# Attention, then two expert layers, on one Trainium2 core: a product's place in the planned order no longer waits for its reciprocals

## The chip, the core and the metric

One core of a Trainium2 chip runs the whole program. PE (TensorE) multiplies, DVE (VectorE), ACT (ScalarE) and POOL (GpSimd) work on tiles, SP (SyncE) issues most transfers. Each engine runs its own instructions in the order in which the program names them. The metric is the device time of one execution in microseconds, the median of the runs.

## The reference

```python
def _attn_ref(q, k, v, tau):          # q, k, v: 4 batches x 8 heads x 576 x 64
    scores = np.matmul(q, k.transpose(0, 1, 3, 2)) / sqrt(64)
    thresh = np.max(scores, axis=-1, keepdims=True) - tau
    scores = np.where(scores >= thresh, scores, -1000000000.0)
    attn = np.exp(scores - np.max(scores, axis=-1, keepdims=True))
    attn = attn / (np.sum(attn, axis=-1, keepdims=True) + 1e-09)
    return np.matmul(attn, v)
def _moe_ref(x, w1, w2, w3, w_out):   # x: 2304 x 512, w1, w2: 512 x 1024
    return ((x @ w1) * (x @ w2) @ w3) @ w_out
def _moe2_ref(x, w_in, w_out):        # w_in: 512 x 2048
    h = x @ w_in
    g = np.where(h > 0.0, h, np.exp(np.minimum(h, 0.0)) - 1.0)
    return g @ w_out
```

The output of the attention, laid out as 2304 tokens of 512 numbers, goes through `_moe_ref`, and that through `_moe2_ref`.

## The kernel before

**Pairs and score tiles.** The 32 heads go in 16 pairs p. The scores of a pair are nine tiles i of 128 rows by 576 columns: positions 0 to 3 make half 0 of the pair (256 rows), positions 4 to 8 half 1 (320 rows), so there are 144 tiles and 32 halves. A name such as `s75` is the score tile 75, and `pv8_1` is the product of pair 8, half 1. Pairs 0 to 3 ("plain") go in another form (L478) and do all their first halves ahead of their second ones.

**A tile's way.** PE makes the scores (`emit_S`, L478 or L490) into one of three PSUM slots `s`. DVE takes each row's maximum (`emit_max`, L500), POOL makes the threshold and the bias of it, ACT the exponential `e` (`emit_exp`, L518), and DVE masks it and sums the rows (`emit_mask`, L524). Then the tile is transposed, in one of two ways, into a buffer `pt` of the half; there are two such buffers. Either PE transposes it back into its own slot and ACT copies that out (`emit_X`, L572; `emit_C`, L576), or ACT and POOL split it into two f16 parts `hl` (L531, L535) and SP starts DMA transposes (`emit_T`, L562 and L564). The second way is taken by second halves from pair 4 on, and by odd pairs below, and by first halves from pair 10 on.

**A half's way.** When its tiles are masked, DVE adds 1e-9 to the row sums and takes reciprocals (`emit_rr`, L584 and L585). PE turns them (`turn_r`, L590, in the slot of the tile named `q + 3` in the code), ACT copies them out (`keep_r`, L595), SP stores them to DRAM (`store_r`, `rd`) and loads them back spread over 64 partitions each (`load_rs`, L615, tile `rb`). When the half's `pt` is full, PE multiplies it with V (`emit_PV`): twelve of the 32 products are in f32 (L629, ten matmuls, each of which the profile counts twice), twenty in f16 (L637, 28 matmuls). DVE multiplies the product with `rb` (`emit_xf`, L646 or L648), ACT and DVE split the result into two parts of x (`emit_xh`, L654; `emit_xl`, L658). The product itself reads V and `pt` only; `rb` is first read by `emit_xf`.

**The first layer's products.** As soon as four pairs of a batch have their x, PE makes `ab` products of them with w1 and w2 (`run_ab`, L679, twelve matmuls each), which ACT (L687) and DVE (L694) evict. Batches 0 to 2 do this among the score tiles; the fourth follows after them. The `ab` products and the products with V share two PSUM banks `m`: a half holds one from the first matmul of its product until `emit_xf`.

**What sets the order.** All of this stage, up to about 420 us, is put in order by a class `Plan`. Each step is an operation with an engine, a modelled duration, a list of steps that must come first, and a key. `run` takes, again and again, the engine that could begin earliest, and on it, among the steps that could begin within `SLACK` of the earliest one, the one with the lowest key. The table `AHEAD` shifts the keys by kind of step and stretch. A step named in a list is thus an entry in the planner's book: the program issues the instructions in the order found, and the semaphores on the chip follow from what each instruction reads and writes, not from the list. The later stages (the matrix M of w3 and w_out, x, h and o with the ELU) are written by hand.

Of the kernel before, what the change touches and what calls it, by code (L numbers as in the profile page):

```python
# [50 lines left out]
SLACK = {"PE": 0.03, "DVE": 0.02, "ACT": 0.05, "POOL": 0.31, "SP": 0.44, "NEW": 0.05}  # L51
AHEAD = {
    ("emit_C", 0, 0): 224.5, ("emit_C", 0, 1): 627, ("emit_C", 1, 1): -173.5, ("emit_C", 1, 2): -182.5,
    ("emit_C", 2, 3): -166, ("emit_C", 2, 4): 48, ("emit_C", 2, 5): -140, ("emit_C", 2, 6): -180,
    ("emit_C", 2, 7): -322, ("emit_H", 1, 1): -184, ("emit_H", 1, 2): -253.5, ("emit_H", 2, 3): 1130,
    ("emit_H", 2, 4): 882, ("emit_H", 2, 5): 1110, ("emit_H", 2, 6): 608.5, ("emit_H", 2, 7): 900,
    ("emit_H", 2, 8): 425, ("emit_H", 2, 9): 950, ("emit_H", 2, 10): 910, ("emit_H", 2, 11): 1090,
    ("emit_L", 1, 1): -91.5, ("emit_L", 1, 2): 43, ("emit_L", 2, 3): 177, ("emit_L", 2, 4): 56.5,
    ("emit_L", 2, 5): 160, ("emit_L", 2, 6): -46.5, ("emit_L", 2, 7): 41.5, ("emit_L", 2, 8): -58,
    ("emit_L", 2, 9): 87.5, ("emit_L", 2, 10): 112, ("emit_L", 2, 11): 316.5, ("emit_PV", 0, 0): -405.5,  # L60
    ("emit_PV", 0, 1): 54.5, ("emit_PV", 0, 2): 23, ("emit_PV", 0, 3): 25, ("emit_PV", 0, 4): -0.5,
    ("emit_PV", 0, 5): 3.5, ("emit_PV", 0, 6): -23.5, ("emit_PV", 0, 7): 76.5, ("emit_PV", 1, 0): -28,
    ("emit_PV", 1, 1): 10.5, ("emit_PV", 1, 2): -84.5, ("emit_PV", 1, 3): -121, ("emit_PV", 1, 4): 2,
    ("emit_PV", 1, 5): -28.5, ("emit_PV", 1, 6): -81.5, ("emit_PV", 1, 7): -16.5, ("emit_S", 0, 0): -362,
    ("emit_S", 0, 1): 20, ("emit_S", 1, 1): -165.5, ("emit_S", 1, 2): -129.5, ("emit_S", 2, 3): -0.5,
    ("emit_S", 2, 4): -255.5, ("emit_S", 2, 5): -113.5, ("emit_S", 2, 6): -27.5, ("emit_S", 2, 7): -3.5,
    ("emit_S", 2, 8): -1.5, ("emit_S", 2, 9): -56, ("emit_S", 2, 10): 5.5, ("emit_S", 2, 11): -116.5,
    ("emit_T", 1, 1): 500.5, ("emit_T", 1, 2): 652.5, ("emit_T", 2, 3): -45.5, ("emit_T", 2, 4): 197,
    ("emit_T", 2, 5): -118.5, ("emit_T", 2, 6): 79.5, ("emit_T", 2, 7): 259.5, ("emit_T", 2, 8): 173,
    ("emit_T", 2, 9): 41.5, ("emit_T", 2, 10): 77.5, ("emit_T", 2, 11): -12, ("emit_X", 0, 0): -360,  # L70
    ("emit_X", 0, 1): -68, ("emit_X", 1, 1): -66.5, ("emit_X", 1, 2): -29.5, ("emit_X", 2, 3): -76.5,
    ("emit_X", 2, 4): -192.5, ("emit_X", 2, 5): -99.5, ("emit_X", 2, 6): -308, ("emit_X", 2, 7): -600,
    ("emit_bias", 0, 0): -141, ("emit_bias", 0, 1): 38, ("emit_bias", 1, 1): -277.5, ("emit_bias", 1, 2): -117,
    ("emit_exp", 0, 0): 154, ("emit_exp", 0, 1): 164.5, ("emit_exp", 1, 1): 53.5, ("emit_exp", 1, 2): -83,
# [192 lines left out]
def attention_moe_moe2(  # L267
# [14 lines left out]
    V, A, G, T, SP = nc.vector, nc.scalar, nc.gpsimd, nc.tensor, nc.sync  # L282
# [442 lines left out]
    call = partial  # L725
# [4 lines left out]
    for i in range(NTILE + 4):  # L730
        p, pos = SEQ[i] if i < NTILE else (NPAIR - 1, 0)
# [745 lines left out]
```

## Time and profile before

| | us |
|---|---|
| runs | 1002.31, 998.86, 996.26 |
| median | 998.86 |
| profiled execution | 1000.01 |
| its span | 998.2 |
| PE busy in the span | 965.1 |

The span is the stretch that the profiler recorded, and 1.8 us of the profiled execution lie around it. PE is busy for nearly all of it, so the time outside of PE's work is 33 us, and most of what remains to be had lies in PE's waits. A timeline row says when a run of like instructions began and how long it took, and in brackets how long the engine was idle ahead of it and what released it.

### The profile page before, as it was taken

The page shows a single profiled execution, that of the slowest core. Times are in us where ns is not written, and L with a number is a line of the kernel's source. Part 1 is how long each engine was busy: PE and PEld are TensorE (multiplying, and loading weights), DVE is VectorE, ACT ScalarE, POOL GpSimd, SP SyncE. Part 2 cuts the span into 40 slices and gives each one's busy share as a digit, 9 for nine tenths or more (in the row PEclk, how much of TensorE's full clock was granted, in tenths as well). Part 3 has the DMA queues.
Part 4 walks back from the last instruction along what each step waited for, and adds up shares of the span by engine and source line. Part 5 has one row for each costly group of instructions (what it writes and reads, how often), then busy time and mean ns, then how long its engine had stood idle before and what let it go on. Part 6 is the DMA issues. An engine that isn't in the chain of part 4 may idle for free. (4 is left out here: it accounts for less than half of the span.)

```text
span 998.2 us, 17869 instructions
## 1 busy us (share of the span) xinstructions
PE 965.1 (97%) x6102; PEld 846.8 (85%) x6102; DVE 719.2 (72%) x1235; ACT 562.5 (56%) x1045; POOL 627.7 (63%) x765
## 2 busy tenths in 40 slices
PE   8889999989999999999999999999999999999998
PEld 5547788768898999999899998898989999899997
DVE  6988876878768878499876664788676656765563
ACT  5777786777666776255444344545555344553442
POOL 3378775776779887255422224878887566875662
PEclk9999999989999999999999999999999999999999
DMA  8437565566898988677758866731215121142201
GB/s 269 149 104 191 137 162 168 147 143 158 186 184 189 200 169 173 180 260 255 244 178 263 291 219 195 257 106 54 64 50 195 57 69 53 49 133 58 69 22 64
DMA packets 182263, 152.51 MB, mean 153 GB/s; under 512 B 119484, under 2 KB 168860, under 8 KB 177564
## 3 DMA queue, kind: packets, MB, share of 16 engines
q1 hardware_dynamic: 178060, 121.72, 45.4%
q10 hardware_dynamic: 4112, 29.66, 8.4%
q8 instruction: 48, 0.79, 0.3%
q14 instruction: 43, 0.35, 0.1%
HBM read 98.89 MB, written 24.72 MB: 124 GB/s over the span
## 5 line engine op out<-in xcount | busy, mean ns | idle before, releaser
L679 PE MATMUL ab<-x,W 128*128 128x256 f32 (+1 forms) x1536 | 223.9, 298 | 3.5 <-ACT a L687 1.7
L1306 PE MATMUL o<-W,gg 128*128 128x512 f32 x864 | 222.8, 390 | 0.0
L679 PEld LDWEIGHTS ab<-x,W 128*128 128x128 f32 x1536 | 207.7, 188 | 12.9 <-issue 6.5
L1215 POOL TENSOR_TENSOR wi<-wr,wi 128x256 fp32r<-128x256 f32 x168 | 144.5, 873 | 65.7 <-ACT wi L1214 53.3
L1306 PEld LDWEIGHTS o<-W,gg 128*128 128x128 f32 x864 | 159.9, 188 | 21.5
L1294 POOL TENSOR_TENSOR gg<-th,gg 128x384 fp32r<-128x384 f32 x96 | 106.4, 1108 | 47.0 <-PE h L1346 26.6
L535 POOL TENSOR_TENSOR hl<-e,hl 128x512 f16<-128x512 f32 x94 | 110.1, 1172 | 30.5 <-ACT hl L531 26.7
L524 DVE SCALAR_TENSOR_TENSOR e<-s,st,e 128x576 f32<-128x576 f32 x144 | 115.1, 809 | 17.5 <-ACT e L518 15.7
L500 DVE TENSOR_REDUCE st<-s 128x1 f32<-128x576 f32 x144 | 106.1, 750 | 19.2 <-PE s L490 8.8
L1346 PE MATMUL h<-sl,wi 128*128 128x384 f32 x576 | 116.6, 338 | 2.3 <-DVE th L1376 1.4
L1288 ACT ACTIVATE et<-et 128x384 f32<-128x384 f32 x96 | 50.1, 522 | 111.8 <-DVE et L1287 111.3
L1346 PEld LDWEIGHTS h<-sl,wi 128*128 128x128 f32 x576 | 102.5, 188 | 11.5 <-DVE th L1376 2.3
L1225 PE MATMUL x<-sl,M 128*128 128x384 f32 x576 | 100.6, 336 | 1.4 <-DVE sl L324 1.4
L1225 PEld LDWEIGHTS x<-sl,M 128*128 128x128 f32 x576 | 99.8, 188 | 2.1 <-DVE sl L324 2.0
L1293 ACT ACTIVATE gg<-th 128x384 fp32r<-128x384 f32 x96 | 50.6, 527 | 77.4 <-DVE th L1291 76.8
L1376 DVE TENSOR_TENSOR th<-h,th 128x384 f32<-128x384 f32 x96 | 53.2, 554 | 56.5 <-PE h L1346 56.3
L1346 PE MATMUL h<-so,wi 128*128 128x384 f32 x432 | 87.4, 337 | 2.4 <-ACT th L1386 1.6
L518 ACT ACTIVATE e<-s,st 128x576 f32<-128x576 f32 x108 | 78.2, 735 | 20.4 <-POOL st L508 14.4
L490 PE MATMUL s<-qk 128*128 128x288 f32 x480 | 84.1, 309 | 4.7 <-DVE e L524 2.5
L1346 PEld LDWEIGHTS h<-so,wi 128*128 128x128 f32 x432 | 76.6, 188 | 10.6 <-ACT th L1386 3.6
L1291 DVE SCALAR_TENSOR_TENSOR th<-et,th 128x384 f32<-128x384 f32 x96 | 72.0, 750 | 16.8 <-ACT et L1288 15.4
L490 PEld LDWEIGHTS s<-qk 128*128 128x128 f32 x480 | 68.9, 191 | 13.6 <-issue 5.1
(113 smaller groups left out, 1515.5 us busy)
## 6 DMA issues: line engine op xcount, KB each, us to landing
wr<-wi_dr SPq DMA_DIRECT2D x168, 128.0 KB
rqk<-in_qk SPq DMA_DIRECT2D x24, 576.0 KB
raw_wo<-in_wo ACTq DMA_DIRECT2D x12, 1024.0 KB
th<-g_dr SPq DMA_DIRECT2D x48, 192.0 KB
raw_w<-in_w SPq DMA_DIRECT2D x8, 1024.0 KB
raw_w<-in_w3t ACTq DMA_DIRECT2D x8, 1024.0 KB
raw_win<-in_win ACTq DMA_DIRECT2D x8, 1024.0 KB
vr<-in_v SPq DMA_DIRECT2D x16, 320.0 KB
```

What stands on the lines that cost most here:

```text
L490: T.matmul(s[:, n, :HS], q, k[:, c:c + HS], start=(x == 0), stop=(x == len(ops) - 1))
L500: V.tensor_reduce(st[i][:, 0:1], sc[i][:, :, :HS], axis=AX.XY, op=ALU.max if plain else ALU.min, negate=plain)
L518: A.activation(et[i], sc[i][:, :, :HS], AF.Exp, bias=st[i][:, k:k + 1], scale=esc if plain else -1.0)
L524: V.scalar_tensor_tensor(et[i], sc[i][:, :, :HS], st[i][:, 1:2], et[i], op0=ALU.is_ge if p < NPL else ALU.is_le, op1=ALU.mult, accum_out=s ...
L535: G.tensor_tensor(t[:, S + 64:], e[:, :512], t[:, :512], op=ALU.subtract)
L679: T.matmul(o[:, :w], wf[:, m, wx, kt, :], x[:, xx, :], start=(kt == 0 and k == 0), stop=(kt == NK - 1 and k == 2),)
L1215: G.tensor_tensor(t[:, 1], r, f32(t[:, 0]), op=ALU.subtract)
L1225: T.matmul(o[:, :TB], M[:, f, mx, e * P:(e + 1) * P], gh[j, f][:, gx, :], start=(k == 0), stop=(k == 23),)
L1291: V.scalar_tensor_tensor(x, c["t"], -1.0, x, op0=ALU.add, op1=ALU.max)
L1294: G.tensor_tensor(h[:, 1, :], x, f32(h[:, 0, :]), op=ALU.subtract)
L1306: T.matmul(po[j, t], dst["h"][:, gx, t * P:(t + 1) * P], WO[f][:, wx, :], start=(first and k == 0), stop=(last and k == 2),)
L1346: T.matmul(o[:, :TB], w[:, wx, kt, :], bs[k][:, kt, xx, :], start=(i == 0), stop=(i == 5),)
```

## The change

One dependency is dropped and the numbers that set the order are searched anew. In the loop over the halves, the first step of `emit_PV` listed `lr`, the spread load of the reciprocals of that half; it no longer does. `emit_xf` still lists it. `SLACK` is zero now for PE, DVE and ACT, larger for POOL and smaller for SP, and nearly every number of `AHEAD` differs; one entry is dropped. No instruction is added or removed.

```diff
-SLACK = {"PE": 0.03, "DVE": 0.02, "ACT": 0.05, "POOL": 0.31, "SP": 0.44, "NEW": 0.05}
+SLACK = {"PE": 0.0, "DVE": 0.0, "ACT": 0.0, "POOL": 0.36, "SP": 0.33, "NEW": 0.05}
 AHEAD = {
...
-    ("emit_L", 2, 9): 87.5, ("emit_L", 2, 10): 112, ("emit_L", 2, 11): 316.5, ("emit_PV", 0, 0): -405.5,
+    ("emit_L", 2, 9): 140.5, ("emit_L", 2, 10): 241.5, ("emit_L", 2, 11): 247.5, ("emit_PV", 0, 0): -449,
...
         pv = v0 = op(
-            call(emit_PV, p, n, 0), VV[p, n] + [x for i in tiles for x in CC[i]] + lr + pvs[-1:], "PE", us[0], q + 5
+            call(emit_PV, p, n, 0), VV[p, n] + [x for i in tiles for x in CC[i]] + pvs[-1:], "PE", us[0], q + 5
         )
```

The instructions move in the stage up to about 420 us, on every engine; from there on the order is the same. The table is a line longer, so a line of the kernel before has a number one higher in the changed kernel. In the rows below a name ends in a running number of the build, which means nothing; `<-` stands between what is written and what is read, and `x4` counts like rows.

On PE, at pair 5: the product `pv5_0`, `ab` products of batch 0, half 1, and transposes of tile 56. Before:

```order
L572 MATMUL s56_1998<-ident_116,e56_2060 128x128 x4
L572 MATMUL s56_1998<-ident_116,e56_2060 64x128
L679 MATMUL ab0_1_3_1_2085<-x0_1_977,W3_578 128x320 x3
L679 MATMUL ab0_1_3_1_2085<-x1_1_1258,W3_578 128x320 x3
L679 MATMUL ab0_1_3_1_2085<-x2_1_1422,W3_578 128x320 x3
L679 MATMUL ab0_1_3_1_2085<-x3_1_1638,W3_578 128x320 x3
L629 MATMUL pv5_0_2102<-pt5_0_1731,vr5_1016 64x256 x10
```

Changed:

```order
L638 MATMUL pv4_1_1839<-pt4_1_1563,v16_4_1167 64x320
L630 MATMUL pv5_0_1927<-pt5_0_1712,vr5_1114 64x256 x4
L491 MATMUL s54_1938<-qk8_742 128x288 x4
L630 MATMUL pv5_0_1927<-pt5_0_1712,vr5_1114 64x256 x2
L491 MATMUL s55_1956<-qk8_742 128x288 x4
L630 MATMUL pv5_0_1927<-pt5_0_1712,vr5_1114 64x256 x4
L491 MATMUL s56_1975<-qk9_889 128x288 x4
L680 MATMUL ab0_1_1_1_1984<-x0_1_1106,W1_373 128x320 x3
```

The product has moved from behind `ab0_1_3_1` and tile 56's transposes to right behind `pv4_1`, in three pieces among the score tiles 54 to 56, and so ahead of five `ab` products.

On DVE, at tile 75, which is the fourth tile of pair 8, half 0: maxima, masks and the reciprocals `rr8_0`. Before:

```order
L500 TENSOR_REDUCE st76_2769<-s76_2753 128x1
L500 TENSOR_REDUCE st77_2773<-s77_2764 128x1
L524 SCALAR_TENSOR_TENSOR e75_2771,sm8_2673<-s75_2738,st75_2760,e75_2771 128x576
L524 SCALAR_TENSOR_TENSOR e76_2778,sm8_2673<-s76_2753,st76_2769,e76_2778 128x576
L524 SCALAR_TENSOR_TENSOR e77_2783,sm8_2673<-s77_2764,st77_2773,e77_2783 128x576
L584 TENSOR_SCALAR rr8_0_2795<-sm8_2673 128x4
```

Changed:

```order
L501 TENSOR_REDUCE st76_2764<-s76_2754 128x1
L525 SCALAR_TENSOR_TENSOR e75_2766,sm8_2659<-s75_2739,st75_2759,e75_2766 128x576
L501 TENSOR_REDUCE st77_2778<-s77_2769 128x1
L585 TENSOR_SCALAR rr8_0_2785<-sm8_2659 128x4
L586 RECIPROCAL rr8_0_2785<-rr8_0_2785 128x4
L525 SCALAR_TENSOR_TENSOR e76_2776,sm8_2659<-s76_2754,st76_2764,e76_2776 128x576
```

The mask of tile 75 now stands ahead of the maximum of tile 77, and the reciprocals ahead of two masks.

On SP, behind the load `rb10_1`: `rqk26` is a load of 576 KB of q and k for a later pair, `hl99` to `hl104` are tiles of pair 11 to be transposed. Before:

```order
L615 DMA rb10_1_3782<-rd10_1_3703 64x320 x2
L394 DMA rqk26_3804<-in_qk 128x1152
L564 DMA_TRANSPOSE pt11_0_3808<-hl99_3716 128x9x128
L564 DMA_TRANSPOSE pt11_0_3808<-hl100_3742 128x9x128
L564 DMA_TRANSPOSE pt11_0_3808<-hl101_3814 128x9x128
```

Changed:

```order
L616 DMA rb10_1_3788<-rd10_1_3704 64x320 x2
L565 DMA_TRANSPOSE pt11_0_3740<-hl99_3752 128x9x128
L565 DMA_TRANSPOSE pt11_0_3740<-hl100_3786 128x9x128
L565 DMA_TRANSPOSE pt11_0_3740<-hl101_3809 128x9x128
L607 DMA rd11_0_3910<-rt11_0_3894 4x128
L565 DMA_TRANSPOSE pt11_0_3740<-hl102_3839 128x9x128
L565 DMA_TRANSPOSE pt11_1_3872<-hl103_3887 128x9x128
L616 DMA rb11_0_3954<-rd11_0_3910 64x256 x2
L699 DMA g_dr_67<-g1_0_0_3811 128x2x256
L565 DMA_TRANSPOSE pt11_1_3872<-hl104_3922 128x9x128
L395 DMA rqk26_3999<-in_qk 128x1152
```

The large load has moved behind six transposes, a store and the spread load of the next half.

## Rows read from the trace of the kernel before

**Rows 1.** The page, part 1: engine, busy us (share of the span), instructions.

```profile
PE 965.1 (97%) x6102; PEld 846.8 (85%) x6102; DVE 719.2 (72%) x1235; ACT 562.5 (56%) x1045; POOL 627.7 (63%) x765
```

**Rows 2.** Windows: stretch; length, busy us (instructions) by engine; PEclk, DMA share, GB/s.

```profile
12.00:32.00 20.00, 18.66 (x139) 11.92 (x137) 17.41 (x32) 15.17 (x22) 7.34 (x17) 1.00 0.70 221
...
52.00:72.00 20.00, 16.33 (x124) 9.10 (x123) 16.74 (x33) 15.59 (x23) 12.93 (x18) 1.00 0.36 119
550.00:1000.00 450.00, 438.38 (x2231) 398.44 (x2229) 288.79 (x441) 210.50 (x469) 288.51 (x286) 1.00 0.34 110
```

**Rows 3.** Tile rb, 10 to 420: what ended idle time (us, times).

```profile
  PE pv L637: 9.0, 8
  PE pv L629: 4.1, 4
  DMA rb<-rd: 1.7, 1
```

**Rows 4.** Timeline, DVE: start, length, line, operation, [idle before <- releaser].

```profile
23.67 0.76 DVE L500 TENSOR_REDUCE st<-s 128x1 f32<-128x576 f32 x1 [1.58 <-PE s L590]
```

**Rows 5.** Timeline, PE: product of pair 0, first half.

```profile
32.69 2.53 PE L629 MATMUL pv<-pt,vr 128*64 128x256 f32 x20
```

**Rows 6.** Timeline, ACT, 160 to 240: copies into pt.

```profile
168.34 1.90 ACT L576 ACTIVATE pt<-s 128x640 f32<-128x640 f32 x3 [4.33 <-PE pv L629]
...
189.99 0.70 ACT L576 ACTIVATE pt<-s 128x640 f32<-128x640 f32 x1 [1.71 <-PE pv L629]
```

**Rows 7.** Timeline, PE, 170 to 200: two waits of score tiles.

```profile
177.05 1.86 PE L490 MATMUL s<-qk 128*128 128x288 f32 x12 [1.02 <-ACT pt L576]
...
192.70 0.80 PE L490 MATMUL s<-qk 128*128 128x288 f32 x4 [0.59 <-ACT pt L576]
```

**Rows 8.** Timeline, PE, 204 to 232: products 6_1 and 7_1, and between.

```profile
204.91 2.09 PE L637 MATMUL pv<-pt,v 128*64 128x320 f16 x28
...
217.06 1.33 PE L572 MATMUL s<-ident,e 128*128 128x128 f32 x5 [1.58 <-DVE e L524]
...
220.41 0.47 PE L637 MATMUL pv<-pt,v 128*64 128x320 f16 x1 [0.61 <-DMA pt<-hl]
221.58 3.89 PE L637 MATMUL pv<-pt,v 128*64 128x320 f16 x27 [0.69 <-DMA pt<-hl]
225.40 3.18 PE L490 MATMUL s<-qk 128*128 128x288 f32 x16
```

**Rows 9.** Timeline, DVE: the third maximum of pair 8.

```profile
215.51 0.76 DVE L500 TENSOR_REDUCE st<-s 128x1 f32<-128x576 f32 x1 [0.30 <-PE s L490]
```

**Rows 10.** Windows: one stretch.

```profile
220.00:225.00 5.00, 3.89 (x28) 3.09 (x28) 1.77 (x3) 1.88 (x4) 4.14 (x6) 0.50 0.75 227
```

**Rows 11.** Timeline, PE: behind the second hole.

```profile
300.10 1.69 PE L679 MATMUL ab<-x,W 128*128 128x256 f32 x12 [1.71 <-ACT a L687]
302.97 2.67 PE L490 MATMUL s<-qk 128*128 128x288 f32 x16 [1.18 <-DVE e L524]
```

**Rows 12.** Timeline, SP: load of rb10_1, then transposes.

```profile
289.97 1.12 SPq L615 DMA_DIRECT2D rb<-rd  x2
...
292.19 6.77 SPq L564 DMA_TRANSPOSE pt<-hl  x3
```

**Rows 13.** Timeline, DVE: xf of product 10_1.

```profile
293.85 0.55 DVE L648 SCALAR_TENSOR_TENSOR xf<-pv,vst,rb 128x320 f32<-128x320 f32 x1 [1.74 <-DMA rb<-rd]
```

**Rows 14.** Timeline, ACT: a copy to f16 (hl).

```profile
298.59 0.68 ACT L531 ACTIVATE hl<-e 128x576 f16<-128x576 f32 x1 [4.25 <-DMA pt<-hl]
```

**Rows 15.** Timeline, PE, 380 to 420: two waits of pairs 14 and 15.

```profile
398.19 1.30 PE L490 MATMUL s<-qk 128*128 128x288 f32 x8 [0.53 <-DVE e L524]
...
416.63 3.64 PE L679 MATMUL ab<-x,W 128*128 128x320 f32 x23 [0.65 <-DVE xf L648]
```

**Rows 16.** Timeline, PE: turn_r of product 9_0.

```profile
244.61 0.27 PE L590 MATMUL s<-ident,rr 128*4 128x128 f32 x1
```

**Rows 17.** Timeline, SP: load of rb9_0.

```profile
247.10 1.10 SPq L615 DMA_DIRECT2D rb<-rd  x2
```

More of the change, by code (lines that the diff above doesn't have):

```diff
@@ new lines @@
+    ("emit_tiny", 0, 1): -24, ("emit_tiny", 1, 1): -204.5, ("emit_tiny", 1, 2): -384, ("emit_tiny", 2, 3): -389.5,
+    ("emit_tiny", 2, 4): -146.5, ("emit_tiny", 2, 5): -193.5, ("emit_tiny", 2, 6): -263.5,
+    ("emit_tiny", 2, 7): -283.5, ("emit_tiny", 2, 8): -390, ("emit_tiny", 2, 9): -500.5,
+    ("emit_tiny", 2, 10): -482.5, ("emit_tiny", 2, 11): 95, ("emit_xf", 0, 0): 313.5, ("emit_xf", 0, 1): 405,
+    ("emit_xf", 0, 2): -228.5, ("emit_xf", 0, 3): -40.5, ("emit_xf", 0, 4): -212.5, ("emit_xf", 0, 5): -127.5,
@@ new lines @@
+    ("emit_xf", 0, 6): -254.5, ("emit_xf", 0, 7): 650, ("emit_xf", 1, 0): 64.5, ("emit_xf", 1, 1): -49,
+    ("emit_xf", 1, 2): 40.5, ("emit_xf", 1, 3): 315, ("emit_xf", 1, 4): 227.5, ("emit_xf", 1, 5): 182,
+    ("emit_xf", 1, 6): 157, ("emit_xf", 1, 7): 272, ("emit_xh", 0, 0): -299.5, ("emit_xh", 0, 1): -105,
+    ("emit_xh", 0, 2): 189.5, ("emit_xh", 0, 3): -414.5, ("emit_xh", 0, 4): -597, ("emit_xh", 0, 5): -625,
+    ("emit_xh", 0, 6): -344.5, ("emit_xh", 0, 7): -101.5, ("emit_xh", 1, 0): -120.5, ("emit_xh", 1, 1): 292,
@@ new lines @@
+    ("load_rs", 1, 3): -106.5, ("load_rs", 1, 4): -121.5, ("load_rs", 1, 5): 31, ("load_rs", 1, 6): 164,
+    ("load_rs", 1, 7): -116, ("load_v", 0): -202, ("load_w", 0): -532, ("low", 0): 488.5, ("new_pt", 0): -547,
+    ("prep_h", 0): -633.5, ("prep_lk", 0): 665, ("prep_lq", 0): -226.5, ("prep_s", 0): 390.5, ("prep_v", 0): 263,
+    ("prep_vl", 0): 188.5, ("rest", 0): 418, ("run_ab", 0, 0): -72, ("run_ab", 0, 1): -47, ("run_ab", 0, 2): 49,
+    ("run_ab", 0, 3): 103.5, ("run_ab", 0, 4): 256.5, ("run_ab", 0, 5): 27, ("run_ab", 0, 6): 166.5,
@@ new lines @@
+    ("run_ab", 0, 7): 41, ("run_ab", 1, 0): 118, ("run_ab", 1, 1): 16.5, ("run_ab", 1, 2): -102,
+    ("run_ab", 1, 3): 59, ("run_ab", 1, 4): 187, ("run_ab", 1, 5): 39.5, ("run_ab", 1, 6): -64.5,
+    ("run_ab", 1, 7): 9.5, ("run_ab", 2, 0): 287.5, ("run_ab", 2, 1): -207.5, ("run_ab", 2, 2): -33,
+    ("run_ab", 2, 3): 134, ("run_ab", 2, 4): -285.5, ("run_ab", 2, 5): 9.5, ("run_ab", 2, 6): -93,
+    ("run_ab", 2, 7): 88, ("sign", 0): 428.5, ("store_g", 0, 0): -200.5, ("store_g", 0, 1): -9.5,
+    ("store_g", 0, 2): -142, ("store_g", 0, 3): -43, ("store_g", 0, 4): 100.5, ("store_g", 0, 5): -52,
@@ new lines @@
+    ("store_r", 0, 2): -480, ("store_r", 0, 3): -416.5, ("store_r", 0, 4): -46, ("store_r", 0, 5): -37,
+    ("store_r", 0, 6): -483.5, ("store_r", 0, 7): -216, ("store_r", 1, 0): -207.5, ("store_r", 1, 1): 111.5,
+    ("store_r", 1, 2): -531, ("store_r", 1, 3): -247.5, ("store_r", 1, 4): 97, ("store_r", 1, 5): -441,
+    ("store_r", 1, 6): -458.5, ("store_r", 1, 7): -199.5, ("top", 0): 433.5, ("turn_r", 0, 0): -627,
+    ("turn_r", 0, 1): -138.5, ("turn_r", 0, 2): -643, ("turn_r", 0, 3): -181, ("turn_r", 0, 4): -128,
@@ L147 @@
+    ("turn_r", 0, 5): -285.5, ("turn_r", 0, 6): -384, ("turn_r", 0, 7): -171, ("turn_r", 1, 0): -384.5,
+    ("turn_r", 1, 1): -221, ("turn_r", 1, 2): -249.5, ("turn_r", 1, 3): -380.5, ("turn_r", 1, 4): -51,
+    ("turn_r", 1, 5): -416, ("turn_r", 1, 6): -275.5, ("turn_r", 1, 7): -386.5, ("v_mean", 0): -549.5,
+    ("v_scale", 0): -338.5, ("v_sum", 0): 154,
 }
```

157 lines of the change are left out of this document (64 added, 93 removed).

## The prediction

> **What bounds the kernel now.** I read the page's busy times first. PE works 965.1 of the span's 998.2 us, DVE 719.2 [rows 1]: the kernel is bound by PE as a whole, and 33.1 us are left in which PE waits. Next, the windows, since an average over stages hides where those 33.1 us are. From 550 to 1000, where the later layers run and the change moves nothing, PE is busy 438.38 of 450, so 11.6 of them lie out of reach. In the attention stage the picture has two parts. From 12 to 72 DVE is the fuller beside PE: in the first 20 us DVE works 17.41 and PE 18.66, in the last 16.74 and 16.33 [rows 2]; PE idles 1.34 and 3.67 us there, and the chain scores, maximum, exponential, mask, transpose sets the pace. After that PE is close to full, and what it loses is in a few holes of 1 to 3 us, which the timelines show one by one. Last, the tile `rb`, which is the one the dropped dependency is about: DVE, at `emit_xf`, waited for a product with V twelve times, 13.1 us in all, and for the reciprocals once, 1.7 us [rows 3]. So in the old order the reciprocals are nearly always there first, and the product is the late one. This is the room that the change can use: a product could start sooner without `emit_xf` having to wait at once.
>
> **What the edit does and doesn't do.** The product never reads `rb`, so no semaphore goes away on the chip; the instructions are the same in number and form, and removal and addition cost nothing. All effect is order. By the two orders, 24 of 32 products stand earlier on PE, mostly by one to four score tiles, seven stand as before, and `pv0_1` stands later. SP's, ACT's and POOL's instructions shift with them, and the new table moves others that have nothing to do with it. I go through the places where PE waits in the old trace and ask of each what stands there now. All terms are against the profiled execution, 1000.01; it lies 1.15 above the median of the runs, 998.86, and since the terms are differences I put them on the median.
>
> **Early part, 12 to 72.** `pv0_0` stood behind tile 10's scores and is now ahead of tile 6's; `pv1_0` to `pv3_0` move likewise. One such product takes 2.53 us [rows 5]. Ahead of `s6` it can delay the maximum of tile 6, for which DVE waited 1.58 us even before [rows 4]; that DVE time is lost for good in a stretch paced by DVE, so the cost is at most the whole 2.53. The other end: products placed earlier fill waits of PE there, at best about half of the 1.34 and 3.67 us of the first and last window, 2.5. No row tells which prevails, since PE's work is the same and DVE has 2.6 and 3.3 us of idle in those windows to absorb a delay. I take **0**, ends −2.5 and +2.5.
>
> **Pairs 5 and 6, 165 to 193.** ACT's copies into `pt` stood 4.33 and 1.71 us behind `pv5_0` and `pv6_0` [rows 6], since there are two `pt` buffers and a copy needs the one that the product still reads. Two later score tiles waited 1.02 and 0.59 for such copies [rows 7]. `pv5_0` now stands five `ab` products earlier and `pv6_0` three and a half `ab` products and two score tiles earlier, so the buffers come free in time. What is late next is DVE, which has few gaps here. Between 0 and −1.6 I take half, **−0.8**.
>
> **Pairs 7 and 8, 214 to 228.** PE waited 1.58 for the mask of tile 75, then 0.61 and 0.69 inside `pv7_1` for transposes to land [rows 8], and the granted clock fell to 0.50, which is 1.2 of 2.4 GHz [rows 10]. On DVE the maximum of tile 77, 0.76 us, stood ahead of that mask and had itself waited 0.30 [rows 9]; the new order puts the mask first, so 0.76 can go. On PE `s79`, four matmuls of 0.80 like the one of [rows 7], now stands ahead of `pv7_1` and fills the first wait, 0.61. But the last transpose lands where it did unless SP is faster, and then the earlier mask only lengthens the wait for it. So: 0.61 and half of 0.76, **−1.0**, ends 0 and −1.4, with the clock falling as before.
>
> **Pairs 10 and 11, 291 to 303.** SP issued a 576 KB load and right behind it three transposes that took 6.77 us [rows 12]; ACT's next copy into `hl` waited 4.25 for them [rows 14], and the eviction of an `ab` product is queued behind that copy on ACT: PE waited 1.71 for it, then 1.18 for a mask [rows 11]. The load now stands behind six transposes. On SP nothing else of it is urgent, as its pair is two pairs away. I take the first wait as gone and the second as staying, because DVE's chain is late next: **−1.7**, ends 0 and −2.9.
>
> **Pairs 14 and 15.** PE waited 0.53 for a slot behind a mask and 0.65 for the last `emit_xf` [rows 15]. `pv14_1` now stands ahead of `s143` and can fill the first, `pv15_1` stands four `ab` products earlier and can remove the second. 0.65 and half of 0.53: **−0.9**, ends 0 and −1.2.
>
> **New waits.** A product that is issued sooner can meet a transpose that has not landed, or a bank that is kept. The nearest row for the first is `pv7_1`, 0.61 and 0.69 [rows 8]. I count one such place, **+1.3**, ends 0 and +4.3 (that place and two bank waits of 1.5, worked out below).
> On this place PE's row shows that score matmuls queued behind `pv7_1` began only when it was through, at 225.40, though their inputs are not the product's [rows 8]. The Trainium skill (TensorE: Matmul & The Clock Gate, Step-by-step: what each phase is for) gives the rule: matmuls stay in program order and only weight loads are pulled ahead. By that rule an early product is no free filler, which speaks against this change; a PE that took the scores first would make this term 0 instead.
>
> **Sum.** 0 − 0.8 − 1.0 − 1.7 − 0.9 + 1.3 = −3.1 us. On the profiled execution 996.9, on the median **995.8**, which is 0.3% faster. A measurement of this kernel can tell about 0.5% from no change, 5.0 us, so the bounds are 993.9 and 1003.9. With its two widest terms at either end the forecast runs from 992.0 to 1001.3; I think 993 to 998 likely.
>
> **Rival A, the clock stays up, 991.1.** If all of 1.58, 0.61 and 0.69 is filled, the hole at 217 is gone, and perhaps the fall of the clock with it. The fall's price is in the rows: `pv7_1` took 0.47 and 3.89 where `pv6_1`, as many matmuls, took 2.09, so 2.27; sixteen score matmuls took 3.18 there [rows 8] and 2.67 at 303 [rows 11], so 0.51. That is 2.8 on top, and the hole gives 2.88 instead of 1.0: 995.8 − 1.9 − 2.8 = 991.1. For it: the places that hold PE here are just the ones that moved. Against it: the landing of the transpose is not moved much, and at 300 PE waited 1.71 and 1.18 with no fall, so the clock does not simply follow one wait. The Trainium skill (same page, What's actually happening) says the throttled clock is the default and activity releases it, which fits a fall behind waits and would come out as this rival if they go. Chance 0.22.
>
> **Rival B, waits only change places, 998.9.** The change does not do what it says it does for time: DVE sets the pace early, `emit_xf` that waited for a product now waits for `rb`, and each filled hole opens one of its size behind it. For it: DVE's shares [rows 2] and that the new table moves much that has nothing to do with products. Against it: 12 of the 13 waits at `rb` were for the product [rows 3]. Chance 0.18.
>
> **Rival C, banks are kept for reciprocals, 1004.9.** The old dependency made sure that a product takes one of the two banks only when its reciprocals are on the way. Take `pv9_0` in the new order: behind `turn_r` stand 4 of 28 matmuls of `pv8_1` (0.30 of the 2.09 in [rows 8]), 3 of 12 of an `ab` product (0.42 of 1.69, [rows 11]), two score tiles (1.60, [rows 7]) and the product (2.53, [rows 5]): it ends 4.85 after `turn_r`. The reciprocals take longer: `turn_r` at 244.61 [rows 16], the load's issue over at 248.20 [rows 17], and up to 2.76 until it lands, by the one time that `emit_xf` waited for it (293.85, [rows 13], against an issue over at 291.09, [rows 12]). That is 6.35, so `emit_xf` waits 1.5 and keeps the bank. By the same count six products past 72 us end within 7 us of their `turn_r` (`pv2_1`, `pv6_0`, `pv9_0`, `pv12_1`, `pv13_0`, `pv14_0`); in the old order each began over 6.6 after it. If each costs PE the 1.74 of the one measured wait [rows 13], that is 10.4; with the four gains of 4.4 lost in it, +6.0. It decides from about six such waits on, (5.0 + 4.4) / 1.74. Against it: while one bank is kept PE has scores to do, and the other bank. Chance 0.15.
>
> **How the numbers follow.** The forecast has 0.45, of which I put 0.08 below 993.9. Faster by over 0.5%: 0.22 of rival A and 0.08, 0.30. Slower by over 0.5%: rival C, 0.15. Within 0.5%: the rest of the forecast and rival B, 0.55. The range should leave out two in ten: from 990.0, just under rival A, where a little of it falls short, to 1003.0, which leaves out most of rival C.
>
> **What would show it.** In the changed profile: ACT's copies near 168 and 190 without their waits of 4.33 and 1.71; tile 75's transpose on PE right behind the scores and `pv7_1` in one piece or with one wait; ACT's 4.25 near 298 gone; at tile `rb`, `emit_xf` released by `rb` several times instead of once, which is the sign of rival C where PE's `ab` rows then show waits for DVE's `xf`. A granted clock of 1.00 through 214 to 228 would mean rival A. The prediction is wrong if PE's busy time changes, which only the clock can do, or if new waits in the early part exceed 2.5.

## The result

The changed kernel takes 1010.05 us, median of six runs, against 999.15 for before in the same session: the ratio is 1.0121, interval 1.0100 to 1.0143. It is 11 us slower, where 3 us faster was forecast. The profiled execution took 1014.23, so its trace shows some 4 us more than the median does; it is set against before's trace, 1000.01.

The page of the changed kernel, part 1, answers [rows 1]:

```profile
PE 969.8 (96%) x6102; PEld 851.7 (84%) x6102; DVE 717.3 (71%) x1235; ACT 563.4 (56%) x1045; POOL 627.6 (62%) x765
```

The span is 1012.4. PE is busy 4.7 us longer with the same instructions, and the time in which it waits has grown from 33.1 to 42.6, by 9.5; the two make the 14.2 us. The windows of the changed kernel show where PE's clock fell (columns as in [rows 2]; the last three are PEclk, DMA share, GB/s):

```profile
0.00:50.00 50.00, 40.31 (x273) 25.13 (x274) 38.59 (x75) 29.90 (x44) 19.30 (x40) 0.97 0.60 188
50.00:100.00 50.00, 45.20 (x316) 29.04 (x316) 39.72 (x73) 34.41 (x50) 34.30 (x51) 0.93 0.51 146
...
150.00:200.00 50.00, 47.86 (x353) 40.75 (x353) 37.71 (x83) 36.50 (x62) 34.05 (x53) 0.97 0.67 162
200.00:250.00 50.00, 45.84 (x359) 37.93 (x359) 38.91 (x86) 36.48 (x61) 34.41 (x54) 1.00 0.65 160
...
300.00:350.00 50.00, 44.52 (x354) 41.83 (x354) 30.64 (x69) 27.92 (x52) 34.76 (x53) 0.93 0.83 166
350.00:400.00 50.00, 47.30 (x391) 43.46 (x387) 37.19 (x84) 34.77 (x62) 42.95 (x65) 0.97 0.77 175
```

Before had one fall in this stage, from 217 to 227 [rows 10]. That one is gone, 200 to 250 reads 1.00, and five others have come: in windows of 2 us the clock is low from 46 to 54, 74 to 78, 158 to 164, 322 to 330 and 354 to 358. PE's waits over 0 to 520 (what waited, for what: us in total, times, longest), of before:

```profile
PE s L572 <- DVE e L524: 5.0, 6, 1.6
PE s L478 <- ACT pt L576: 4.4, 7, 1.3
PE s L490 <- DVE e L524: 2.5, 5, 1.2
...
PE s L490 <- ACT pt L576: 1.9, 3, 1.0
PE ab L679 <- ACT a L687: 1.7, 1, 1.7
PE pv L637 <- DMA pt<-hl: 1.3, 2, 0.7
...
PE ab L679 <- DVE g L694: 1.0, 2, 0.5
PE ab L679 <- DVE xf L648: 0.6, 1, 0.6
PE s L478 <- DVE e L524: 0.5, 1, 0.5
```

and of the changed kernel, whose line numbers are one higher:

```profile
PE s L573 <- DVE e L525: 8.9, 8, 2.5
PE pv L638 <- DMA pt<-hl: 3.7, 7, 0.8
PE s L479 <- ACT pt L577: 3.5, 7, 0.8
PE pv L638 <- DMA rqk<-in_qk: 3.4, 1, 3.4
...
PE pv L638 <- DVE st L501: 2.0, 1, 2.0
PE pv L638 <- ACT a L688: 2.0, 2, 1.7
PE s L491 <- DVE e L525: 1.7, 5, 0.6
PE pv L638 <- DVE e L525: 1.5, 1, 1.5
PE s L491 <- ACT pt L577: 1.1, 2, 0.8
...
PE ab L680 <- DVE g L695: 0.5, 1, 0.5
```

Added up by what waited: products with V 1.3 before and 12.6 now, transposes on PE 5.0 and 8.9, scores 9.3 and 6.3, `ab` products 3.3 and 0.5. That is +11.3, +3.9, −3.0 and −2.8, or +9.4, the whole growth of the idle time. The releasers of the five kinds of product waits differ. The 2.0 us put down to ACT may be waits for a bank, which its evictions of `ab` products free. For the others, a wait for several things is put down to the one that came last by the profile, and a product reads no mask, no maximum and not that load, which is for a later pair; the places, below, point to the transposes. At tile `rb` the new trace reads (answering [rows 3]):

```profile
  PE pv L638: 5.8, 5
  DMA rb<-rd: 1.7, 3
  PE pv L630: 0.5, 2
```

`emit_xf` waited for reciprocals three times, 1.7 us in all, as much as in the one wait of before. So the loss is not there.

The three products that lost most are in PE's timeline of the changed kernel. First `pv4_1`, whose first six matmuls stand ahead of the scores of tile 51:

```profile
156.89 0.30 PE L638 MATMUL pv<-pt,v 128*64 128x320 f16 x1 [1.52 <-DVE e L525]
157.81 0.59 PE L638 MATMUL pv<-pt,v 128*64 128x320 f16 x5 [0.62 <-DMA pt<-hl]
158.33 0.80 PE L491 MATMUL s<-qk 128*128 128x288 f32 x4
```

Then `pv11_1` and `pv12_1`, in the same timeline further on:

```profile
324.00 4.43 PE L638 MATMUL pv<-pt,v 128*64 128x320 f16 x28 [3.40 <-DMA rqk<-in_qk]
...
354.00 3.96 PE L638 MATMUL pv<-pt,v 128*64 128x320 f16 x28 [2.00 <-DVE st L501]
```

Scores are queued behind each of them. Next, the last transposes of `pv4_1`'s half, tile 44, in SP's timeline of before (start, length of the issue):

```profile
138.64 2.54 SPq L562 DMA_TRANSPOSE pt<-hl  x2
```

and those of `pv11_1`'s half, tile 107, there:

```profile
312.24 2.54 SPq L562 DMA_TRANSPOSE pt<-hl  x2
```

Tile 44's in SP's timeline of the changed kernel:

```profile
153.70 2.59 SPq L563 DMA_TRANSPOSE pt<-hl  x2
```

and tile 107's there, with the load ahead of it:

```profile
318.96 0.45 SPq L395 DMA_DIRECT2D rqk<-in_qk  x1
319.51 2.56 SPq L563 DMA_TRANSPOSE pt<-hl  x2
```

In PE's timeline of before, `pv4_1` is this row:

```profile
151.17 2.09 PE L637 MATMUL pv<-pt,v 128*64 128x320 f16 x28
```

and `pv11_1` begins with this one:

```profile
322.77 1.00 PE L637 MATMUL pv<-pt,v 128*64 128x320 f16 x12
```

So the issue of the last transpose had been over for 10.0 and 8.0 us when the product began. In the changed kernel it was over for 0.6 and 1.9 us, after waits. This is not only the product's doing: `pv11_1` begins at about the same time in both traces, 322.77 and 324.00, and it is the transposes that have become late. In SP's order, tile 44's transposes stood ahead of the store and the spread load of that half's own reciprocals and now stand behind both; tile 107's stood ahead of that store and now stand behind it, behind a store of g and behind the 576 KB load `rqk27` (318.96 above). While the product had to wait for its reciprocals in the plan, it could not come sooner than a store and a load after the last mask, and the transposes of the same mask were through by then. So I read the entry, which nothing on the chip needed, as the room that the transposes had. This is read off the two orders; the runs below don't show it, and one speaks against it.

### The profile page after: what moved, and what is told of

It is laid out like the page before. It is cut to its first block, busy times and chain, and to the rows that moved or that the text cites. A ratio compares the mean times of both kernels' runs of the same rounds, so it can differ in the third digit from the quotient of the medians.

```text
span 1012.4 us, 17878 instructions
## 1 busy us (share of the span) xinstructions
PE 969.8 (96%) x6102; PEld 851.7 (84%) x6102; DVE 717.3 (71%) x1235; ACT 563.4 (56%) x1045; POOL 627.6 (62%) x765
## 4 chain that ended last, share of the span: by engine, by line
PE 70%; DVE 9%; DMA 6%; issue 5%; ACT 5%; POOL 4%; SPq 1%; ACTq 0%; DVEq 0%; POOLq 0%
PE o L1307 17%; PE h L1347 15%; PE ab L680 13%; PE x L1226 8%; PE m L1016 4%; PE s L491 4%; PE pv L638 3%; DMA pt<-hl 3%; PE s L479 2%; DVE e L525 2%; PE pv L630 2%; POOL hl L536 2%; PE s L573 2%; ACT e L519 1%; DVE st L501 1%
```

## The experiments

All ratios are to before on the same chip in the same session. For kernels with an order of their own, the search is left and its steps are issued from a list; their line numbers are 104 above before's:

```diff
-            o.fn()
...
+        for k in ORDER:
+            self.ops[k].fn()
```

**The two halves of the change.** `edit_only` is the dropped entry with the old numbers, `table_only` the new numbers with the entry:

```diff
 edit_only, against before:
-            call(emit_PV, p, n, 0), VV[p, n] + [x for i in tiles for x in CC[i]] + lr + pvs[-1:], "PE", us[0], q + 5
+            call(emit_PV, p, n, 0), VV[p, n] + [x for i in tiles for x in CC[i]] + pvs[-1:], "PE", us[0], q + 5
 table_only, against the changed kernel:
-            call(emit_PV, p, n, 0), VV[p, n] + [x for i in tiles for x in CC[i]] + pvs[-1:], "PE", us[0], q + 5
+            call(emit_PV, p, n, 0), VV[p, n] + [x for i in tiles for x in CC[i]] + lr + pvs[-1:], "PE", us[0], q + 5
```

> The dropped dependency alone, with the numbers of before. Theory M (margins: what costs is that products with V are issued before their last transposes have landed, pv4_1, pv11_1 and pv12_1 above all): these three stand early here too, by 4, 6 and 6 us of PE work, so this is 7 to 12 us slower than before, and PE's waits of products at L637 for transposes are some 8 us or more against 1.3. Theory N (it is the new numbers that cost, by what they move on SP, POOL and in the early part): within 3 us of before.

> The new numbers with the dependency put back. Theory M: the products are held back again, so within 3 us of before, and the waits of products for transposes are under 3 us. Theory N: 7 to 14 us slower than before, with the load rqk27 still right ahead of the transposes of tile 107.

Measured: 1.0319 (1.0267 to 1.0370) and 1.0398 (1.0363 to 1.0434). Both theories missed. Either half alone is about three times as bad as the two together, so the loss can't be shared out between them; it looks as if the numbers fit only the plan that they were searched with. In `edit_only` PE waited 5.4 us in products and 18.6 for masks (transposes and scores), so products are not its main loss. In `table_only`, where the entry is back, products waited 10.4 us, nearly all of it for transposes and once for 6.7. So the entry by itself does not keep a product behind its transposes. What drives these two was not followed further.

**By stretch.** Orders of before and of the changed kernel were put together at the scores of a tile:

```diff
 ORDER, with c the step emit_S of that tile
+ head_before: before up to c=56, then changed
+ mid_after:   before up to 56, changed up to 112, then before
+ head_after:  changed up to 26, then before
+ pair4_after: before up to 30, changed up to 57, then before
+ tail_after:  before up to 110, then changed
```

> The order of before up to the scores of tile 56 (about 163 us), from there the order of the changed kernel. The changed kernel runs 13.9 us behind before at this point and 14.2 at the end, with gains of 10 and losses of 14 in between. If stretches are independent, this is 0.4 us slower than before, 999.5. If the losses past 317 us come from the lateness that the early part hands on (its transfers against PE's work), they go too and it is about 10 us faster than before, 989.

> The order of before up to the scores of tile 56, the changed kernel's from there to the scores of tile 112 (about 318 us), and before's again behind. In the changed kernel this middle stretch gained 10.4 us on before (13.9 behind at its start, 3.5 at its end). If stretches are independent, this is 10 us faster than before, 989. If the gain was only a catching up, in waits that before doesn't have, it is within 3 us of before.

> The order of the changed kernel up to the scores of tile 26 (about 82 us), before's order behind. The changed kernel is 6.9 us behind before there. If the early part is a cause by itself: 5 to 8 us slower than before, with the granted clock falling around 45 and 75 us. If before's order behind has the room to catch up: within 2 us of before.

> Before's order up to the scores of tile 30 (about 94 us), the changed kernel's from there to the scores of tile 57, before's behind: this holds pv4_1 ahead of its transposes and the earlier pv5_0. If that product is a cause by itself: 3 to 7 us slower than before, with the wait of pv4_1 of 1.5 us or more in the trace and the clock falling near 157. If the wait there came from the lateness of SP that the early part left: within 2 us of before.

> Before's order up to the scores of tile 110 (about 312 us), the changed kernel's behind: this holds pv11_1 and pv12_1 ahead of their transposes, with the loads rqk26 and rqk27 where before has them. If the products are the cause of the losses from 317 to 341: 6 to 12 us slower than before. If it takes the loads that the changed kernel has put off (a transpose or POOL behind a late 576 KB load): within 3 us of before.

| | ratio | interval |
|---|---|---|
| head_before | 1.0037 | 1.0015 to 1.0059 |
| mid_after | 1.0015 | 0.9996 to 1.0033 |
| head_after | 1.0077 | 1.0050 to 1.0103 |
| pair4_after | 1.0058 | 1.0041 to 1.0075 |
| tail_after | 1.0069 | 1.0044 to 1.0095 |

Three stretches each cost by themselves, seams included: 7.7, 5.8 and 6.9 us. Two thirds of the whole loss goes with the order up to tile 56. The three add up to 20, the change to 12, so the stretch between gives something back; `mid_after` doesn't show it by itself, and its seams at tiles 56 and 112 add waits of 1.1 and 2.6 us of their own, so the size of this stays open. `tail_after` has `rqk26` and `rqk27` where before has them and loses all the same, which speaks against the put-off loads as the only cause there.

In `pair4_after` the wait of `pv4_1` is there though PE was only about 1 us behind before at 144 us, by the work done (PE's timeline):

```profile
150.61 0.30 PE L741 MATMUL pv<-pt,v 128*64 128x320 f16 x1 [0.96 <-DVE e L628]
151.84 0.78 PE L741 MATMUL pv<-pt,v 128*64 128x320 f16 x5 [0.93 <-DMA pt<-hl]
```

**The products alone, both ways.** `late_pv` takes the three products back in the changed kernel, `early2` puts two of them early in before's order, and `head_pv11` takes `pv11_1` back in `head_before`:

```diff
 late_pv, PE, in the changed order (pieces of a product in brackets)
- pv4_1[0] s51 turn_r5_0 v_mean5 s52 s53 pv4_1[1:5]
+ s51 turn_r5_0 v_mean5 s52 s53 pv4_1[0:5]
- pv11_0[0] pv11_1 s114 s115 pv11_0[1:5] s116 ab1_0_6_0
+ pv11_0[0] s114 s115 pv11_0[1:5] s116 ab1_0_6_0 pv11_1
- pv12_1 ab2_1_2_0 s121 s122 s123
+ ab2_1_2_0 s121 s122 pv12_1 s123
 head_pv11: the second of these, in head_before
 early2, PE, in before's order
- s51 turn_r5_0 v_mean5 s52 s53 pv4_1[0:5]
+ pv4_1[0] s51 turn_r5_0 v_mean5 s52 s53 pv4_1[1:5]
- s114 ab1_0_6_1 ab1_0_7_0 turn_r12_0 pv11_1[0:2] s115 pv11_1[2:5]
+ pv11_1 s114 ab1_0_6_1 ab1_0_7_0 turn_r12_0 s115
```

> The changed kernel with three products later on PE and nothing else moved: the first piece of pv4_1 behind the scores of tile 53 (it stood ahead of tile 51's), pv11_1 behind pv11_0 and ab1_0_6_0, pv12_1 behind the scores of tile 122 (it stood ahead of tile 121's). Theory M (products issued before their transposes have landed): the waits of 0.6 to 3.4 us there and the fall of the clock behind them go, and with them most of the 7.1 lost at 155 and of the 12.5 lost from 317 to 341: 10 to 16 us faster than the changed kernel, about 997. Theory L (late loads on SP delay the transposes, whatever stands ahead): PE waits in the next product or score instead, at most 4 us faster, 1006 or more.

> Before's order with two products earlier on PE, where the changed kernel has them, and nothing else moved: the first piece of pv4_1 ahead of the scores of tile 51 (2.3 us of PE work earlier), pv11_1 ahead of tile 114's (6 us earlier). Before issued their last transposes 10.0 and 8.0 us ahead of them. Theory M (what costs is the wait for a transpose that has not landed, not the early place): no wait over 0.5 at either, within 2 us of before. If an early product costs by the scores that it pushes back: 3 us or more slower than before, without waits of products.

> Before's order up to the scores of tile 56, the changed kernel's behind, and in it pv11_1 behind ab1_0_6_0 (it stood inside pv11_0). The kernel without this last move was 0.37% slower than before and lost 7.3 us between 317 and 352, of which pv11_1's wait for tile 107 began it. If the product's wait is the cause: 4 to 6 us less, 994 to 996, faster than before. If a score waits for its mask there instead: as without the move, 1000.

Measured: `late_pv` 1.0120 (1.0091 to 1.0148), `early2` 0.9990 (0.9969 to 1.0011), `head_pv11` 1.0035 (1.0017 to 1.0054). An early place costs nothing where the transposes are early. In `early2` both products start without a wait, 7.5 and 4.7 us after the issue of their last transposes; the second in PE's timeline:

```profile
314.17 2.09 PE L741 MATMUL pv<-pt,v 128*64 128x320 f16 x28
```

But taking the products back doesn't return the time. In `late_pv` and `head_pv11` scores wait for masks at the same places. PE's timeline of `late_pv`:

```profile
319.76 1.79 PE L594 MATMUL s<-qk 128*128 128x288 f32 x8 [2.82 <-DVE e L628]
...
355.29 1.30 PE L594 MATMUL s<-qk 128*128 128x288 f32 x4 [2.50 <-DVE e L628]
```

and of `head_pv11`:

```profile
314.01 2.26 PE L594 MATMUL s<-qk 128*128 128x288 f32 x8 [3.75 <-DVE e L628]
```

So the wait in front of the product is where the loss is seen, and not shown to be its cause. What is late there is the chain that feeds the masks. In `head_pv11` POOL's first step on the put-off load `rqk26` waits 1.76 for it at 306.25, POOL's bias stands behind that step, and ACT's exponential waits 2.38 for the bias at 312.27. The changed kernel has the same wait on POOL:

```profile
317.12 0.75 POOL L398 TENSOR_SCALAR rqk<-rqk,esc 128x576 f32<-128x576 f32 x1 [2.67 <-DMA rqk<-in_qk]
```

It can't be all: in `tail_after`, with the load early, PE still waits 2.38 for a mask at 315.30.

**The loads, and the early products.**

```diff
 loads_back, SP, in the changed order
+ rqk26 ahead of T101, rqk27 ahead of T105
- rqk26 behind T104, rqk27 ahead of T107
 early_pv, PE, in the changed order
+ pv0_0 behind s10, pv1_0 behind s13, pv2_0 ahead of s17, pv3_0 behind X17
- pv0_0 ahead of s6, pv1_0 behind s10, pv2_0 around s15 and s16, pv3_0 around X16
 all3: late_pv, early_pv and loads_back together
```

> The changed kernel with two 576 KB loads earlier on SP and nothing else moved: rqk26 ahead of the transpose of tile 101 (it stood behind that of 104), rqk27 ahead of that of 105 (it stood right ahead of that of 107). Theory L: pv11_1 no longer waits 3.4 us for tile 107, and the clock does not fall behind it: 5 to 7 us faster than the changed kernel. Theory M: the product still comes before its last transpose has landed, by 1 us or more, and it is within 3 us of the changed kernel.

> The changed kernel with the four first products later on PE and nothing else moved: pv0_0 behind the scores of tile 10 (it stood ahead of tile 6's), pv1_0 behind tile 13's, pv2_0 ahead of tile 17's, in one piece, pv3_0 behind the transposes of tile 17. The changed kernel is 6.9 us behind before at 82 us. If the early products are the cause, by holding up the maximum of tile 6 (DVE waited 2.83 there against 1.58), this is 4 to 7 us faster than the changed kernel. If it is what the new numbers moved on DVE and POOL (a split of x on DVE took 2.35 us at 42.8 instead of 0.41), it is within 2 us of it.

> All of the three edits before (three products late, four early products late, two loads earlier) in the changed kernel. If each takes away what it is meant for and the middle stretch keeps its gain of 10 us, this is faster than before: 1010 less 14, less 6, 990. If the middle stretch only caught up what had been lost ahead of it, as in the kernel made of before, changed and before again (0.15% slower than before), it is 996 to 1000.

Measured: 1.0197 (1.0167 to 1.0227), 1.0224 (1.0189 to 1.0259) and 1.0301 (1.0269 to 1.0333). All three are slower than the changed kernel; none of the expectations held. `loads_back` does not test the late loads. Its wait on SP, from 296 to 310, and PE's in the next `ab` product, from 0 to 520, are these (engine and line, what it waited for: us, times, longest):

```profile
SPq L498 <- POOL qk L522: 6.2, 1, 6.2
...
PE ab L783 <- ACT a L791: 6.2, 1, 6.2
```

The buffer that `rqk26` goes into was still to be read by POOL, so SP stood still ahead of the load with the transposes queued behind it; ACT's next copy into `hl` waited 7.33 for them, and the eviction that PE needs stands behind that copy. `all3` has the same order on SP and a wait of 6.3 there. Whether the late loads cause the loss past 312 was thus not settled. In the early part DVE's order counts on the early products: `emit_xf` stands where the early product has its result, and with the products moved back DVE waited there 3.44, 3.49 and 1.85 us in `early_pv`.

**The early part on DVE and POOL.** DVE's timeline of the changed kernel at the split of x of `pv1_0`:

```profile
42.76 2.35 DVE L659 TENSOR_TENSOR x<-xf,x 128x256 fp32r<-128x256 f32 x1
```

POOL's beside it:

```profile
42.49 2.34 POOL L360 TENSOR_TENSOR W<-w_w,W 128x1024 fp32r<-128x1024 f32 x1
```

and PE's behind:

```profile
45.90 0.76 PE L573 MATMUL s<-ident,e 128*128 128x128 f32 x5 [2.27 <-DVE e L525]
47.46 2.19 PE L479 MATMUL s<-qkp 128*64 128x288 f32 x8 [0.79 <-ACT pt L577]
```

The split takes 2.35 us instead of the 0.41 that the one at 35.29 took. It begins 0.27 behind POOL's operation and ends 0.28 behind it. The mask behind it is late, PE waits 2.27, and the eight score matmuls behind take 2.19 instead of 1.19: the granted clock reads 0.50 from 48 to 52, which is the lower of PE's two levels, 1.2 instead of 2.4 GHz. The Trainium skill (SBUF — State Buffer, Who interferes with whom) says that DVE and POOL share one pair of ports as an exclusive lock, held for the whole instruction. The trace agrees: the 2.35 stands beside POOL's 2.34.

```diff
 xl_late, DVE, in the changed order
- xl1_0 mask11
+ mask11 xl1_0
 xl_prep: the same, and on POOL
- prep_lq8 bias20 bias21 tiny20 tiny21
+ bias20 bias21 tiny20 tiny21 prep_lq8
```

> The changed kernel with one instruction moved on DVE: the split xl1_0 behind the mask of tile 11 (it stood ahead of it). In the changed kernel this split took 2.35 us instead of 0.41 while POOL ran a 2.34 us operation, the mask came late, PE waited 2.27 for it and the clock fell behind. If that is the cause of the early loss: PE's wait at 46 under 0.5, no fall of the clock there, 2 to 4 us faster than the changed kernel. If the split only passes its delay to what stands behind it: the same as the changed kernel.

> The changed kernel with xl1_0 behind the mask of tile 11 on DVE, and on POOL the preparation of q of head 8 behind the small steps of tiles 20 and 21 (it stood ahead of them, took 1.41 us, and DVE's mask of tile 20 waited 1.41 for POOL). With the first of these alone it was 0.94% slower than before, against 1.21%. If the second wait of the early part comes from POOL's order: PE's wait of 2.2 us near 73 falls under 1 and the clock holds there, 1 to 3 us faster than with the first alone. If it only moves behind: the same as with the first alone.

Measured: 1.0094 (1.0072 to 1.0115) and 1.0099 (1.0060 to 1.0138). In `xl_late` PE's wait at the place falls to 0.71 (its timeline):

```profile
44.28 0.76 PE L676 MATMUL s<-ident,e 128*128 128x128 f32 x5 [0.71 <-DVE e L628]
47.24 2.19 PE L582 MATMUL s<-qkp 128*64 128x288 f32 x8 [2.20 <-ACT pt L680]
```

but the next scores wait 2.20 for a copy and still run at the lower clock. By the ratios the first move is worth some 0.27% of the change's 1.21%, with intervals that overlap, and the second nothing that can be told: in `xl_prep` the wait near 73 fell only from 2.17 to 1.56, and though the clock held there, it fell at 320 instead. The rest of the 7.7 us of the early part was not found.

**The terms of the prediction, one at a time,** in before's order:

```diff
 t3, DVE
- max77 mask75
+ mask75 max77
 t3, PE
- pv7_1 s79
+ s79 pv7_1
 t4, SP
- rqk26 T99 T100 T101
+ T99 T100 T101 rqk26
 t3_early2: t3 and early2 together
```

> Before's order with the two moves at pairs 7 and 8 that the prediction costed, alone: the mask of tile 75 ahead of the maximum of tile 77 on DVE, the scores of tile 79 ahead of pv7_1 on PE. By the prediction's step: 1.0 us faster than before, 0 to 1.4; if the fall of the clock behind the hole goes too, 3 to 5 us faster, with a granted clock of 1.00 from 214 to 228.

> Before's order with the load rqk26 behind the transpose of tile 101 on SP (it stood ahead of tile 99's), alone. By the prediction's step: PE's waits of 1.71 and 1.18 at 300 shrink, 1.7 us faster than before. If the delay only moves (POOL's and ACT's preparation of rqk26 then comes late for the scores of pair 13 and what is queued behind it): PE waits 2 to 3 us near 315 for a mask, as in the kernel that went back to before's order at tile 112, and it is within 1.5 us of before or slower.

> Before's order with the moves of two runs that were not slower: the mask of tile 75 and the scores of tile 79 earlier (0.19% faster alone), pv4_1's first piece and pv11_1 earlier (0.10% faster alone, within its interval). If the two add: 2 to 3 us faster than before, 0.2 to 0.3%. If the hole at 214 only comes back elsewhere: within 1 us of before.

Measured: `t3` 0.9981 (0.9961 to 1.0000), `t4` 1.0001 (0.9980 to 1.0023), `t3_early2` 1.0002 (0.9979 to 1.0025). In `t4` the transposes go out sooner and the wait of 1.71 for ACT at 300 [rows 11] is gone. In its place stands this row of POOL's timeline:

```profile
300.07 0.75 POOL L501 TENSOR_SCALAR rqk<-rqk,esc 128x576 f32<-128x576 f32 x1 [2.70 <-DMA rqk<-in_qk]
```

and this one of PE's:

```profile
302.76 1.81 PE L594 MATMUL s<-qk 128*128 128x288 f32 x8 [2.27 <-DVE e L628]
```

POOL's first step on the later load waits 2.70 for it, the bias of the next tile is queued behind that step, and PE waits 2.27 for the mask that needs it, where before it waited 1.18. No kernel was found that is faster than before beyond its interval; `t3`, whose interval ends at 1.0000, comes nearest.

## Why the prediction was wrong

**New waits: +1.3, ends 0 and +4.3. Measured +11.3.** This step failed. I counted one place like `pv7_1`, and took its size from the rows, but I did not look how far each product stood from its own last transpose. The trace of before and the two orders had it: 10.0 us for `pv4_1`, and on SP the transposes of tile 44 moved behind a store and two loads. I followed one load on SP and not the transposes themselves. The +11.3 is where PE's waits stand in the trace; what makes the transposes late was not shown, and holding three products back returned nothing (`late_pv`). Rival C had the direction right, but not the mechanism: three waits for `rb` instead of six, 1.7 us instead of 10.4.

**Early part: 0, ends −2.5 and +2.5. Measured 7.7 slower alone (`head_after`, 5.0 to 10.3 by its interval).** This step failed too, and an experiment has it alone. I took DVE's 2.6 and 3.3 us of idle time as enough to absorb a delay. PE's idle time up to 90 us grew from 11.6 to 14.5, by 2.9, more than the 2.5 that I had named as a sign of being wrong, and the clock fell twice, which I had priced at nothing. The cause that I gave, `pv0_0` ahead of `s6`, is small: DVE's wait there went from 1.58 to 2.83. What I left out is DVE's and POOL's own order and the clock; how much each of them costs stays open.

**Pairs 5 and 6: −0.8.** ACT's waits of 4.33 and 1.71 are gone as expected, and PE has no wait from 165 to 215, so both of its waits for copies went, 1.6. Not tried alone.

**Pairs 7 and 8: −1.0, ends 0 and −1.4. Measured 1.9 faster alone, 0 to 3.9 (`t3`).** The size is right within what can be told, the mechanism is not. PE's waits in the hole shrank only from 3.14 to 2.93. From the start of `pv6_1` to the `ab` products behind the hole the traces take 23.5 and 22.5 us, so most of the 1.0 between them came with the clock, which fell in `t3` too, but for a shorter time. In the changed kernel and in `t3_early2` it held. That is the sign that I gave for rival A, but its condition did not come true: the changed kernel still waits 3.43 us there. Nor did its time: the changed kernel lost the clock at five other places, and `t3_early2` is no faster than before.

**Pairs 10 and 11: −1.7. Measured 0.0, ±2.1 (`t4`).** I wrote that nothing else of the load was urgent on SP. That was so on SP, but not on POOL, whose next steps in order wait for the load. In the changed kernel both waits at 300 are gone, and POOL waits 2.67 for that load at 317.

**Pairs 14 and 15: −0.9.** The wait of 0.53 is 0.43 in the new trace. That of 0.65 for the last `emit_xf` is gone as expected, but a new one of 0.39 for reciprocals to turn stands at 406, so about 0.4 of the term is left.

**Sum of the gains.** Scores and `ab` products wait 5.8 less, near the 4.4 that I had added up, but in part by luck: nothing came at pairs 7 and 8, and at the two other large terms more than I took. These gains are outweighed more than twice over by the products' and the transposes' waits, with 4.7 us of a lower clock on top.

**What stays open:** why either half of the change alone costs 30 to 40 us, what makes up the rest of the early loss, what makes the masks and transposes late past 312, and how much the stretch from tile 57 to 110 gives back. So the cause of the loss as a whole is not shown; the runs show in which stretches it arises.

## What to carry to other kernels

Before dropping a dependency from a planner because the data doesn't need it, find out what else it holds in place: list for each step that it held back the next-latest input, and how long that had been there (10 and 8 us here, 0.6 and 1.9 after). That shows where waits will come; no run here shows that moving the step back removes the loss. A step that is put off on one queue must be followed to every engine on which something stands behind its consumer, POOL here. A load that is taken forward must be checked for who still reads its buffer (6.2 us on SP in `loads_back`). And numbers found by search seem to belong to the plan that they were searched with: seven variations of the changed kernel, in one part or a few, ran from 0.9 to 4% slower than before, and none was beyond doubt better than it.

## What the runs showed of the hardware

PE's clock does not simply follow the length of its waits. Before kept it behind waits of 1.71 and 1.18 at 300 [rows 11]; the changed kernel lost it behind 2.27 and 0.79 at 45. In `t3` and `t3_early2` the hole at 214 has nearly the same waits, 1.13, 0.73, 0.49 and 0.31 in the one and 1.12, 0.72, 0.49, 0.69 and 0.38 in the other. Behind them, 27 matmuls of `pv7_1` took this in PE's timeline of `t3`:

```profile
220.44 3.89 PE L741 MATMUL pv<-pt,v 128*64 128x320 f16 x27 [0.31 <-DMA pt<-hl]
```

and this in that of `t3_early2`:

```profile
220.09 2.06 PE L741 MATMUL pv<-pt,v 128*64 128x320 f16 x27 [0.38 <-DMA pt<-hl]
```

So a fall, and the 2 us that it costs here, can't be read from single waits ahead of the run. Nor does the order alone decide it: up to 140 us `t3_early2` has before's order, and behind the same waits at 50 (1.27, 0.46, then 0.43 against 0.63) its clock fell from 50 to 56, where before's held. Which falls a trace shows is thus in part a matter of the one execution that was traced, and so is how the changed kernel's 4.7 us divide.
